# Reordering the units between the chained products of a two-layer MLP (adaLN, linear attention, Mish)

## The chip, the cores and the metric

The kernel runs on one core of a Trainium2 chip. The metric is the device time of one execution in microseconds (us), smaller being better. The engines are called PE (TensorE, matrix products), DVE (VectorE), ACT (ScalarE), POOL (GpSimd) and SP (SyncE, which only starts transfers here); each takes its instructions in the order in which the program wrote them.

## The reference

One sequence of S = 2048 rows with D = 512 columns; c is one row of 512, and silu(c) @ w_mod gives six rows of modulation (sa, ca, ga, sb, cb, gb).

```python
h = layernorm(x) * (1 + ca) + sa
x = x + ga * A(h)        # linear attention, 32 heads of 16, then wo
h = layernorm(x) * (1 + cb) + sb
x = x + gb * B(h)        # B: mish(h @ w1 + b1) @ w2, w1 512 x 1792, w2 1792 x 512
```

Everything is float32. The change touches only the second half, B, and the order of work around it.

## The kernel before, in words

**Precision.** Each float32 operand is split into a high half (fp32r) and the low rest, and a product is three matmuls: high x high, high x low, low x high (`mm3`). `split` makes the halves: ACT copies the high half (L75), and one step later DVE subtracts it from the value to give the low half (L81).

**Tiling.** The rows of x are four blocks of 512 (0 to 3). The 1792 hidden columns are 14 column tiles f of 128, taken as seven pairs g = (2g, 2g+1).

**Products of a pair.** The first layer is computed for two row blocks and the two column tiles of a pair at once, with seven products in place of eight (Strassen's scheme in Winograd's form, in the names of w1's quarters a11 .. a22, their sums s1 .. s4, the inputs' quarters b11 .. b22 and their sums t1 .. t4). One `product` (L924) is 6 matmuls of 128 x 512. Four of them accumulate one on the other in one PSUM bank `pa`, and between two of them ACT copies the bank out, so that they form a chain:

- `pair_begin`: a11 x b11 into pa (ACT copies it to u1, L940); a12 x b21 into a second bank, and DVE adds u1 to give c11 (L935).
- `pair_unit`: s1 x t1 into pc; s2 x t2 onto pa, copied to u2 (L962); s3 x t3 onto pa, copied to u3 (L967), and c22 = pc + u3; a22 x t4 onto pa, from which ACT takes mish directly (L899); s4 x b22 onto pc, and c12 = pc + u2.

A product "onto pa" can't start before ACT has copied the bank. Therefore `pair_unit` has two gaps, one ahead of s3 x t3 and one ahead of a22 x t4, in which it calls other PE work (`between[0]`, `between[1]`).

**Mish.** Of the four results of a pair, c11 and the one from pa belong to the first of the two blocks (`mish`: L899, then a split into the halves a_h and a_l), c22 and c12 to the second (`later`, `mish_b`: L922).

**Second layer.** In the first pair stage (blocks 0 and 1), `d_unit(0, f)` is the second layer of block 0 for column tile f: 12 matmuls of 128 x 512 onto four banks `oacc` (L67 to L69). `trail(f)` wraps it. The gaps of pair g hold trail(2g-1) and trail(2g), so the second of them uses the c11 of its own pair; pair 0 has an output unit of the attention, `o_unit(3, 3)`, in its first gap; trail(13) comes last. Then `second(1)` does the 14 d_units of block 1. In the last stage (blocks 2 and 3, pairs in the order 5, 6, 0, 1, 2, 3, 4) the second layer is again in seven products; `e_unit(c, n)` (12 matmuls of 256 columns) for c = 0 and 1 are the first two, and run in the gaps: e_unit(1, n-1) in the first gap of pair n, e_unit(0, n) in its second. The other products (`seventh`: m4, m6, m7, m5, m3) follow the pairs.

**The order of work.** PE's order is written out by hand. Side work is a set of generators: `spawn` adds one, and each `tick()` lets every generator do one step, in the order in which they were spawned; so the instructions of ACT, DVE, POOL and SP come between PE's at the ticks. The ones that matter here:

- `rows(g, wait)` (L588): the w1 rows of pair g. Step 1 starts two SP loads `w1p` (L593); `wait` steps later DVE makes the sums s1 to s4 (L599 to L602); then the high halves on ACT and the low halves on DVE, over three steps.
- `store_rows(g)` (L621): eight SP stores of these halves, for the last stage.
- `w2_job(f)` (L520): an SP load `w2r` (L518), after two steps DVE multiplies by gb (L526), then a split, then two or three POOL stores.
- `norm_tile(b, t)` (L764): the second layer norm of 128 rows of blocks 2 and 3. Two passes of sums on ACT (L213, L214); a step later DVE adds eps (L218) and POOL takes the power -1/2 (L192); a step later DVE makes nb (L222) and ACT applies the norm (L201); a step later POOL stores the tile.

Tiles in SBUF come from one ring of 101 slots, so a new tile also waits until the last reader of its slot is done.

**Where they are spawned before.** In the loop over the first stage's pairs: `w2_job(2g+2)` and `w2_job(2g+3)` at the head of pair g; a norm tile at the head of pairs 1 to 4 and in trails 0, 1, 3, 5, so that no pair has over two; `store_rows(g)` right after pair g, and behind it `rows(g+2, 2)`.

Of the kernel before, what the change touches and what calls it, by code (L numbers as in the profile page):

```python
# [10 lines left out]
AF = mybir.ActivationFunctionType  # L11
# [6 lines left out]
NB = S // 512  # L18
NF = F // P
# [6 lines left out]
def block_kernel(ctx: ExitStack, tc: tile.TileContext, x, wqkv, wo, w1, b1t, w2, c, wmodt, out):  # L26
# [76 lines left out]
    c0 = sb("c0")  # L103
# [408 lines left out]
    KEPT, SUMS_KEPT = 5, (3, 4)  # L512
# [75 lines left out]
    def rows(g, wait):  # L588

        r = [sb(f"w1p_{g}_{i}", F32, (P, 4, P)) for i in range(2)]  # L590
        for i in range(2):
            f = 2 * g + i
            sp.dma_start(r[i], w1[:, P * f:P * (f + 1)].rearrange("(k p) f -> p k f", p=P))  # L593
        for _ in range(wait):
            yield
        a11, a12, a21, a22 = [r[i][:, 2 * k:2 * k + 2, :] for i in range(2) for k in range(2)]
        s12, s34 = [sb(f"s{n}_{g}", F32, (P, 4, P)) for n in (12, 34)]
        s1, s2, s3, s4 = s12[:, 0:2, :], s12[:, 2:4, :], s34[:, 0:2, :], s34[:, 2:4, :]
        dve.tensor_tensor(s1, a21, a22, op=ALU.add)  # L599
        dve.tensor_tensor(s2, s1, a11, op=ALU.subtract)  # L600
        dve.tensor_tensor(s3, a11, a21, op=ALU.subtract)
        dve.tensor_tensor(s4, a12, s2, op=ALU.subtract)  # L602
        yield
        keep, todo = {}, []
        op_rows[g] = keep
        for name, v, parts in (("a1", r[0], ("a11", "a12")), ("s12", s12, ("s1", "s2")), ("s34", s34, ("s3", "s4")),
                               ("a22", a22, ("a22",))):
            half = split(f"{name}_{g}", v, keep, name)
            next(half)
            todo.append((name, half, parts))  # L610
            if len(todo) == 2:
# [113 lines left out]
    def o_unit(b, t, tag="acc"):  # L725
        p = ps(tag, f"o_{b}_{t}")
        ts = slice(P * t, P * (t + 1))
        for g in range(4):
            mm3(p, [q[:, ts] for q in qs[b, g]], ms[g], g == 0, g == 3)
        spawn(o_post(p, b, t))  # L730
# [166 lines left out]
    def mish(p, b, f):  # L897
        u = ua[f] = sb(f"u_{b}_{f}")
        act.activation(u, p, AF.Mish, bias=b1c[:, f:f + 1])  # L899
        yield from split(f"a_{b}_{f}", u, ag, (b, f))  # L900
# [23 lines left out]
    def product(g, left, right, tag="h", onto=None):  # L924

        p = onto if onto is not None else ps(tag, f"p_{left}_{g}")
        for c in range(2):
            a, b = [h[:, c, :] for h in op_a[g, left]], op_b[right, c]
            for i, (st, mv) in enumerate(((a[0], b[0]), (a[0], b[1]), (a[1], b[0]))):
                pe.matmul(p, st, mv, start=onto is None and c == 0 and i == 0, stop=c == 1 and i == 2,  # L930
                          skip_group_check=onto is not None)
        return p
# [4 lines left out]
    def pair_begin(c0, g, tags):  # L937

        u1, pa = sb(f"u1_{g}"), product(g, "a11", "b11", tags[0])
        act.activation(u1, pa, AF.Copy)  # L940
        c11 = sb(f"c11_{g}")
        add(c11, product(g, "a12", "b21", tags[1]), u1)
        return pa, c11

    def later(p, f, wait=0):
        for _ in range(wait):
            yield
        mish_b(p, f)
        yield

    def pair_unit(c0, g, between, begun=None, tags=("tp", "h", "h")):


        f = 2 * g
        u2, u3, c12, c22 = [sb(f"{n}_{g}") for n in ("u2", "u3", "c12", "c22")]
        if begun is None:
            begun = pair_begin(c0, g, tags)
            tick()
        pa, c11 = begun
        pc = product(g, "s1", "t1", tags[2])  # L960
        product(g, "s2", "t2", onto=pa)
        act.activation(u2, pa, AF.Copy)  # L962
        spawn(mish(c11, c0, f))
        tick()
        between[0]()
        product(g, "s3", "t3", onto=pa)
        act.activation(u3, pa, AF.Copy)  # L967
        add(c22, pc, u3)
        spawn(later(c22, f + 1))
        between[1]()  # L970
        m = mish(product(g, "a22", "t4", onto=pa), c0, f + 1)
        next(m)
        spawn(m)
        product(g, "s4", "b22", onto=pc)
        add(c12, pc, u2)
        spawn(later(c12, f, 1))
        tick()

    def prep_a(b, f):
        yield from split(f"a_{b}_{f}", ub.pop(f), ag, (b, f))  # L980
# [11 lines left out]
    def ahead(b, u):  # L992

        if 0 <= u - NF + 4 < NF and last_first[u - NF + 4] < 2 * KEPT:
            w2_again(last_first[u - NF + 4])
        if 0 <= u - NF + 3 < NF:
            spawn(prep_a(b, last_first[u - NF + 3]))
# [17 lines left out]
            load_wb(6)  # L1015


    def tags_of(n):
        return "tp" if n % 2 else "h", "h", "h"

    begun = {g: pair_begin(0, g, ("tp" if g else "h", "acc")) for g in range(2)}
    tick()
    o_unit(NB - 1, 2)
    tick()
    tiles = [norm_tile(b, t) for b in (2, 3) for t in range(4)]

    def trail(f):
        def unit():
            if tiles and (f == 0 or f % 2):
                spawn(tiles.pop(0))  # L1030
            d_unit(0, f, f)
            ahead(1, f)
            tick()
        return unit

    def last_o():
        o_unit(NB - 1, 3)
        tick()

    for g in range(G):  # L1040
        for f in (2 * g + 2, 2 * g + 3) if g < G - 1 else ():
            spawn(w2_job(f))
        if g == 0:
            spawn(rows(2, 3))
        if g and tiles:
            spawn(tiles.pop(0))
        pair_unit(0, g, (trail(2 * g - 1) if g else last_o, trail(2 * g)), begun.get(g), tags_of(g))
        if g < G - 2:
            store_rows(g)
        if 0 < g < G - 2:  # L1050
            spawn(rows(g + 2, 2))
        if g == G - 1:
            for n in range(8):
                load_back("n", nd, 2 + n // 4, n % 4)
    trail(NF - 1)()
    second(1, prepare)


# [45 lines left out]
    def left_trail(g):  # L1104
        yield
        yield
        yield from left_sums(g)
# [45 lines left out]
        else:  # L1153
            pool.dma_start(v, w2t[g][:, :, SUM[name], :])  # L1154

    begun = {}

    def begin_next():
        begun[1] = pair_begin(L, pairs[1], ("tp", "acc"))

    for n, g in enumerate(pairs):
        if n < 5:
            if n:
                load_rows(n)
            if n:
                load_wb(pairs[n + 1])
        if n == 5:
            load_wb(pairs[6])
            load_r(0, 0)
        if n == 6:  # L1170
            for m in pairs[:5]:
                load_wt("m4", m)
        def first(n=n):
            if n == 0:
                begin_next()
            else:
                e_unit(1, n - 1)
            tick()

        def second_gap(n=n):  # L1180
            e_unit(0, n)
            tick()

        pair_unit(L, g, (first, second_gap), begun.pop(n, None), tags_of(n))
        if n < EARLY:
            spawn(left_trail(g))

    names = ["m4", "m6", "m7", "m5", "m3"]
    units = [(name, n) for name in names for n in range(G)]
# [5 lines left out]
    for k, (name, n) in enumerate(units[:4 * G]):  # L1195
        for _ in range(2 if k in (6, 10, 14, 18) else 1):
            if ahead_of:
                nm, m = ahead_of.pop(0)
                spawn(left_prep(nm, pairs[m]))
        for _ in range(2 if k < 3 else 1):  # L1200
            if loads:
                nm, m = loads.pop(0)
                load_wt(nm, pairs[m])
        if k in (3, 8):
            load_r(k // 8, 1)
        seventh(name, tags[name], left.pop((name, pairs[n])), wt.pop((name, pairs[n])), n, G - 1)
        if n == G - 1:
            spawn(finish(name))
        tick()
        if k == 1:  # L1210
            e_unit(1, G - 1)
            spawn(finish("m2"))
            tick()
# [42 lines left out]
```

## Time and profile before

| | us |
|---|---|
| runs | 513.6, 514.48, 513.16 |
| median of the runs | 513.6 |
| profiled execution | 513.23 |
| its span | 511.4 |
| first pair stage, first product to first d_unit of block 1 | 203.36 to 324.85 |
| PE busy in the span | 493.9 |

The span runs from the first to the last instruction that the profiler recorded; the execution's own time is 1.8 us longer. Times inside the kernel are given in us from the span's start. A row of the waits view gives the engine, the waiting instruction's output and line, what released it, and the us in total, how often, and the longest. A row of the timeline gives start, duration, engine, line, operation, output and inputs, and in brackets the idle time before it and what ended that. A row of the windows view gives the stretch and its length, then the busy us of PE, PE's weight loads, DVE, ACT and POOL, the clock granted to PE, the share of time in which the DMA engines were busy, and GB/s. Matmuls are pipelined: one lasts 0.39 us in the timeline, but the next starts 0.23 us after it. Names in the rows are cut before the first number: a_2h stands for a high half named a..._2..., of w1's quarter of pair 2 as well as of a hidden tile 2.

### The profile page before, as it was taken

The numbers are of one execution on the slowest core, as the hardware profiler recorded it, in microseconds if no ns is written. First come the engines' busy times: TensorE is split into PE (matmuls) and PEld (weight loads), VectorE is DVE, ScalarE is ACT, GpSimd is POOL, SyncE is SP. The second block draws the span as 40 slices with busy tenths as digits, with TensorE's granted clock in tenths as the row PEclk, the third lists the DMA queues.
The fourth block names the chain that finished last, engine by engine and source line by source line (L and its number), as shares of the span: only waits on it lengthen the run. The fifth ranks groups of instructions, "written<-read, shape, count | busy, mean of one in ns | idle before, by whom it ended". The sixth has DMA issues, their size and how long they took to land.

```text
span 511.4 us, 7692 instructions
## 1 busy us (share of the span) xinstructions
PE 493.9 (97%) x2648; PEld 412.1 (81%) x2648; DVE 344.2 (67%) x666; ACT 295.0 (58%) x532; POOL 145.1 (28%) x246
## 2 busy tenths in 40 slices
PE   7999999999999999998999999999989999999997
PEld 6788888878788888786777778788778888899997
DVE  6896564878888679864476543779944655549862
ACT  6868683634455977457877554468245444467200
POOL 3573020000223133122533204124364231355200
PEclk9999999999999999999999999999999999999999
DMA  8724661562735135869999619879997463587612
GB/s 298 279 82 84 185 142 64 159 233 83 185 91 164 32 113 182 286 226 347 297 301 309 219 46 348 262 215 370 364 320 212 115 166 82 139 223 198 161 43 83
DMA packets 66765, 98.58 MB, mean 193 GB/s; under 512 B 7405, under 2 KB 31861, under 8 KB 66726
## 3 DMA queue, kind: packets, MB, share of 16 engines
q0 software_dynamic: 29360, 45.31, 32.2%
q1 hardware_dynamic: 37220, 52.51, 31.1%
q8 instruction: 21, 0.34, 0.3%
q10 hardware_dynamic: 146, 0.26, 0.1%
q14 instruction: 18, 0.15, 0.1%
HBM read 62.92 MB, written 33.03 MB: 188 GB/s over the span
## 4 chain that ended last, share of the span: by engine, by line
PE 81%; ACT 6%; DVE 4%; issue 4%; DMA 2%; POOL 1%; DVEq 0%; POOLq 0%; ACTq 0%
PE p_a L930 15%; PE p_s L930 6%; PE oacc L69 4%; PE oacc L68 4%; PE oacc L67 4%; PE m L69 4%; PE m L68 3%; PE m L67 3%; PE pq L67 3%; PE gacc L68 3%; PE gacc L69 3%; PE gacc L67 3%; PE pq L69 3%; PE pq L68 3%; PE o L67 3%
## 5 line engine op out<-in xcount | busy, mean ns | idle before, releaser
L935 DVE TENSOR_TENSOR c<-p_s,u 128x512 f32<-128x512 f32 x28 | 19.4, 691 | 51.6 <-PE p_s L930 33.7
L962 ACT ACTIVATE u<-p_a 128x512 f32<-128x512 f32 x14 | 8.4, 597 | 32.5 <-PE p_a L930 32.3
L922 ACT ACTIVATE ub<-c,b1c 128x512 f32<-128x512 f32 x28 | 20.1, 718 | 9.0 <-DVE c L935 9.0
L192 POOL TENSOR_TENSOR rs_n<-rs_n,half 128x1 f32<-128x1 f32 x16 | 10.8, 676 | 37.0 <-DVE rs_n L218 26.2
L1154 POOL DMA_DIRECT2D wt_m<-w2t x20 | 14.0, 704 | 25.4 <-PE p_a L930 17.3
L248 DVE SCALAR_TENSOR_TENSOR ku<-e_k,relu_k 128x512 f32<-128x512 f32 x16 | 11.0, 689 | 14.5 <-ACT relu_k L246 14.5
L586 POOL DMA_DIRECT2D w2b<-w2d x20 | 10.6, 534 | 29.5 <-PE oacc L69 8.3
L245 ACT ACTIVATE e_q<-pq 128x512 f32<-128x512 f32 x16 | 9.4, 590 | 16.5 <-PE pq L69 16.5
L788 ACT ACTIVATE hf_n<-tp_n,mc 128x512 f32<-128x512 f32 x16 | 11.7, 770 | 11.2 <-PE tp_n L786 11.2
L940 ACT ACTIVATE u<-p_a 128x512 f32<-128x512 f32 x14 | 8.3, 593 | 15.6 <-PE p_a L930 15.6
L245 ACT ACTIVATE e_k<-pk 128x512 f32<-128x512 f32 x16 | 9.6, 599 | 13.3 <-PE pk L69 13.2
L935 DVE TENSOR_TENSOR c<-p_a,u 128x512 f32<-128x512 f32 x14 | 9.7, 690 | 8.6 <-ACT u L940 5.8
L899 ACT ACTIVATE u<-p_a,b1c 128x512 f32<-128x512 f32 x14 | 9.6, 686 | 10.1 <-PE p_a L930 8.5
L694 POOL DMA_DIRECT2D rden_d<-rden x3 | 2.2, 718 | 43.4 <-DVE rden L692 43.4
L248 DVE SCALAR_TENSOR_TENSOR q<-e_q,relu_q 128x512 f32<-128x512 f32 x16 | 11.0, 688 | 4.7 <-ACT relu_q L246 4.5
L967 ACT ACTIVATE u<-p_a 128x512 f32<-128x512 f32 x14 | 8.3, 594 | 10.1 <-PE p_a L930 10.1
L580 POOL DMA_DIRECT2D wb<-w2d x14 | 9.9, 711 | 14.7 <-PE p_a L930 9.3
L201 ACT ACTIVATE x<-x,nb_x,rs_x 128x512 f32<-128x512 f32 x15 | 11.5, 810 | 3.8 <-DVE nb_x L196 3.3
L192 POOL TENSOR_TENSOR rs_x<-rs_x,half 128x1 f32<-128x1 f32 (+1 forms) x10 | 7.4, 746 | 21.2 <-DVE rs_x L187 20.4
L201 ACT ACTIVATE r<-r,nb_n,rs_n 128x512 f32<-128x512 f32 x8 | 6.5, 812 | 10.7 <-DVE nb_n L222 8.9
L718 DVE TENSOR_TENSOR r<-o,r 128x512 f32<-128x512 f32 x16 | 10.9, 679 | 2.6 <-PE o L69 2.3
L706 DVE SCALAR_TENSOR_TENSOR q<-q,rd 128x512 f32<-128x512 f32 x16 | 10.6, 686 | 2.6 <-DMA rd<-rden_d 2.5
(1426 smaller groups left out, 1941.4 us busy)
## 6 DMA issues: line engine op xcount, KB each, us to landing
wm<-in_wmodt_dram SPq DMA_DIRECT2D x24, 256.0 KB, 4.5
w2b<-w2d POOLq DMA_DIRECT2D x20, 256.0 KB, 6.1
wt_m<-w2t POOLq DMA_DIRECT2D x20, 256.0 KB, 4.0
r<-in_x_dram SPq DMA_DIRECT2D x16, 256.0 KB, 2.9
x<-in_x_dram SPq DMA_DIRECT2D x15, 256.0 KB, 4.7
w1p<-in_w_dram SPq DMA_DIRECT2D x14, 256.0 KB, 5.0
w2r<-in_w_dram SPq DMA_DIRECT2D x14, 256.0 KB, 5.3
wb<-w2d POOLq DMA_DIRECT2D x14, 256.0 KB, 4.5
```

Source lines behind the costliest of these rows:

```text
L67: pe.matmul(o, st[0], mv[0], start=start, stop=False)
L68: pe.matmul(o, st[0], mv[1], start=False, stop=False)
L69: pe.matmul(o, st[1], mv[0], start=False, stop=stop)
L192: pool.tensor_tensor(y, y, half[:, lo:hi], op=ALU.pow)
L201: act.activation(dst, t, AF.Identity, bias=nb[key, b][:, j:j + 1], scale=rs[key, b][:, j:j + 1])
L245: act.activation(e, p, AF.Exp)
L248: dve.scalar_tensor_tensor(dst, e, 1.0, r, op0=ALU.min, op1=ALU.add)
L788: act.activation(hf[b, j], p, AF.Identity, bias=mc[:, 12 + j:13 + j], scale=mc[:, 16 + j:17 + j])
L922: act.activation(u, p, AF.Mish, bias=b1c[:, f:f + 1])
L930: pe.matmul(p, st, mv, start=onto is None and c == 0 and i == 0, stop=c == 1 and i == 2, skip_group_check=onto is not None)
L935: dve.tensor_tensor(out, p, u, op=ALU.add)
L1154: pool.dma_start(v, w2t[g][:, :, SUM[name], :])
```

## The change

It has three parts.

**Units one pair back.** `pair_unit` is cut into `pair_early` (s1t1, s2t2), `pair_middle` (s3t3) and `pair_end` (a22t4, s4b22). In the first pair stage the gaps of pair g hold trail(2g-3) and trail(2g-2); trails 11, 12 and 13 come after pair 6. In the last stage the gaps of pair n hold e_unit(0, n-1) and e_unit(1, n-1), and the two e_units of the last pair run after the second of the `seventh` products.

**The first two pairs in turns.** In both stages the first two pairs (0 and 1, and 5 and 6) run in `two_pairs`, after the four products of their two `pair_begin`: s1t1 and s2t2 of the first, s1t1 of the second, s3t3 of the first, s2t2 of the second, a22t4 and s4b22 of the first, [e_unit(0, 0)], s3t3 of the second, [trail(0), or e_unit(1, 0)], a22t4 and s4b22 of the second. Between two products of one chain there is here a single product of the other pair, apart from the last gap. In the first stage both o_units stand ahead of this.

**Side work.** `rows(g+2, 2)` is spawned in the second gap of pair g, behind the d_unit, two steps sooner than before. `store_rows(0)` and `store_rows(1)` both follow `two_pairs`, 16 SP stores in a row. `w2_job(2g)` and `w2_job(2g+1)` are spawned at the head of pair g instead of a pair sooner, except those of pair 1, which keep their place. A norm tile is spawned at the head of each pair and in each trail until there are none left: two in `two_pairs`, three in pair 2, three in pair 3.

Every instruction of before is still there, and none is added; only their order changes.

```diff
-    def pair_unit(c0, g, between, begun=None, tags=("tp", "h", "h")):
...
+    def pair_early(c0, g, pa, c11, tag):
+
+        u2 = sb(f"u2_{g}")
+        pc = product(g, "s1", "t1", tag)
         product(g, "s2", "t2", onto=pa)
         act.activation(u2, pa, AF.Copy)
-        spawn(mish(c11, c0, f))
-        tick()
-        between[0]()
+        spawn(mish(c11, c0, 2 * g))
+        return pa, pc, u2
+
+    def pair_middle(g, pa, pc, u2):
+        u3, c22 = sb(f"u3_{g}"), sb(f"c22_{g}")
         product(g, "s3", "t3", onto=pa)
         act.activation(u3, pa, AF.Copy)
         add(c22, pc, u3)
-        spawn(later(c22, f + 1))
-        between[1]()
-        m = mish(product(g, "a22", "t4", onto=pa), c0, f + 1)
+        spawn(later(c22, 2 * g + 1))
+
+    def pair_end(c0, g, pa, pc, u2):
+        c12 = sb(f"c12_{g}")
+        m = mish(product(g, "a22", "t4", onto=pa), c0, 2 * g + 1)
         next(m)
         spawn(m)
         product(g, "s4", "b22", onto=pc)
         add(c12, pc, u2)
-        spawn(later(c12, f, 1))
-        tick()
+        spawn(later(c12, 2 * g, 1))
+        tick()
+
+    def pair_unit(c0, g, odd, between):
+        begun = pair_begin(c0, g, ("tp" if odd else "h", "h"))
+        tick()
+        state = pair_early(c0, g, *begun, "h")
+        tick()
+        between[0]()
+        pair_middle(g, *state)
+        between[1]()
+        pair_end(c0, g, *state)
+
+    def two_pairs(c0, g0, g1, begun, between):
+
+        s0 = pair_early(c0, g0, *begun[0], "h")
+        tick()
+        pc = product(g1, "s1", "t1", "h")
+        pair_middle(g0, *s0)
+        tick()
+        pa, c11 = begun[1]
+        u2 = sb(f"u2_{g1}")
+        product(g1, "s2", "t2", onto=pa)
+        act.activation(u2, pa, AF.Copy)
+        spawn(mish(c11, c0, 2 * g1))
+        tick()
+        pair_end(c0, g0, *s0)
+        between[0]()
+        pair_middle(g1, pa, pc, u2)
+        between[1]()
+        pair_end(c0, g1, pa, pc, u2)
...
+    begun = [pair_begin(0, g, ("tp" if g else "h", "acc")) for g in range(2)]
     tick()
-    o_unit(NB - 1, 2)
-    tick()
+    for t in (2, 3):
+        o_unit(NB - 1, t)
+        tick()
...
-    def trail(f):
+    def norm_next():
+        if tiles:
+            spawn(tiles.pop(0))
+
+    def trail(f, side=None):
         def unit():
-            if tiles and (f == 0 or f % 2):
-                spawn(tiles.pop(0))
+            norm_next()
             d_unit(0, f, f)
             ahead(1, f)
+            if side is not None:
+                spawn(side)
             tick()
         return unit
...
-    for g in range(G):
-        for f in (2 * g + 2, 2 * g + 3) if g < G - 1 else ():
+    for g in range(1, G):
+        for f in (2 * g, 2 * g + 1):
             spawn(w2_job(f))
-        if g == 0:
+        if g == 1:
             spawn(rows(2, 3))
-        if g and tiles:
-            spawn(tiles.pop(0))
-        pair_unit(0, g, (trail(2 * g - 1) if g else last_o, trail(2 * g)), begun.get(g), tags_of(g))
-        if g < G - 2:
+            norm_next()
+            two_pairs(0, 0, 1, begun, (tick, trail(0, rows(3, 2))))
+            store_rows(0)
+        else:
+            norm_next()
+            pair_unit(0, g, g % 2, (trail(2 * g - 3), trail(2 * g - 2, rows(g + 2, 2) if g + 2 < G else None)))
+        if g < KEPT:
             store_rows(g)
-        if 0 < g < G - 2:
-            spawn(rows(g + 2, 2))
...
-    trail(NF - 1)()
+    for f in (NF - 3, NF - 2, NF - 1):
+        trail(f)()
     second(1, prepare)
...
-        pair_unit(L, g, (first, second_gap), begun.pop(n, None), tags_of(n))
-        if n < EARLY:
-            spawn(left_trail(g))
+        if n == 0:
+            begun = [pair_begin(L, pairs[i], ("tp" if i else "h", "acc")) for i in range(2)]
+            tick()
+        elif n == 1:
+            two_pairs(L, pairs[0], g, begun, (gap(0, 0), gap(1, 0)))
+            for i in range(2):
+                spawn(left_trail(pairs[i]))
+        else:
+            pair_unit(L, g, n % 2, (gap(0, n - 1), gap(1, n - 1)))
+            if n < EARLY:
+                spawn(left_trail(g))
...
         if k == 1:
+            e_unit(0, G - 1)
             e_unit(1, G - 1)
             spawn(finish("m2"))
             tick()
```

More of the change, by code (lines that the diff above doesn't have):

```diff
@@ L949, in later @@
         yield
-    def pair_unit(c0, g, between, begun=None, tags=("tp", "h", "h")):
[L954 to L957, printed above, removed]
-            tick()
-        pa, c11 = begun
-        pc = product(g, "s1", "t1", tags[2])
+    def pair_early(c0, g, pa, c11, tag):
+        u2 = sb(f"u2_{g}")
+        pc = product(g, "s1", "t1", tag)
         product(g, "s2", "t2", onto=pa)
         act.activation(u2, pa, AF.Copy)
-        spawn(mish(c11, c0, f))
-        tick()
-        between[0]()
+        spawn(mish(c11, c0, 2 * g))
+        return pa, pc, u2
+    def pair_middle(g, pa, pc, u2):
+        u3, c22 = sb(f"u3_{g}"), sb(f"c22_{g}")
         product(g, "s3", "t3", onto=pa)
@@ L1015, in prepare @@
             load_wb(6)
-    def tags_of(n):
-        return "tp" if n % 2 else "h", "h", "h"
-    begun = {g: pair_begin(0, g, ("tp" if g else "h", "acc")) for g in range(2)}
+    begun = [pair_begin(0, g, ("tp" if g else "h", "acc")) for g in range(2)]
     tick()
-    o_unit(NB - 1, 2)
-    tick()
+    for t in (2, 3):
+        o_unit(NB - 1, t)
+        tick()
     tiles = [norm_tile(b, t) for b in (2, 3) for t in range(4)]
-    def trail(f):
+    def norm_next():
+        if tiles:
+            spawn(tiles.pop(0))
+    def trail(f, side=None):
         def unit():
-            if tiles and (f == 0 or f % 2):
-                spawn(tiles.pop(0))
+            norm_next()
             d_unit(0, f, f)
             ahead(1, f)
+            if side is not None:
+                spawn(side)
             tick()
         return unit
-    def last_o():
-        o_unit(NB - 1, 3)
-        tick()
-    for g in range(G):
-        for f in (2 * g + 2, 2 * g + 3) if g < G - 1 else ():
+    for g in range(1, G):
+        for f in (2 * g, 2 * g + 1):
             spawn(w2_job(f))
-        if g == 0:
+        if g == 1:
             spawn(rows(2, 3))
-        if g and tiles:
-            spawn(tiles.pop(0))
-        pair_unit(0, g, (trail(2 * g - 1) if g else last_o, trail(2 * g)), begun.get(g), tags_of(g))
-        if g < G - 2:
+            norm_next()
[5 more added lines that the diff above has]
+        if g < KEPT:
             store_rows(g)
-        if 0 < g < G - 2:
-            spawn(rows(g + 2, 2))
         if g == G - 1:
@@ L1154, in load_wt @@
             pool.dma_start(v, w2t[g][:, :, SUM[name], :])
-    begun = {}
-    def begin_next():
-        begun[1] = pair_begin(L, pairs[1], ("tp", "acc"))
     for n, g in enumerate(pairs):
@@ L1172, in block_kernel, with gap, unit @@
                 load_wt("m4", m)
[L1173 to L1177, printed above, removed]
-            tick()
-        def second_gap(n=n):
-            e_unit(0, n)
-            tick()
-        pair_unit(L, g, (first, second_gap), begun.pop(n, None), tags_of(n))
-        if n < EARLY:
-            spawn(left_trail(g))
+        def gap(c, m):
+            def unit():
+                if m >= 0:
+                    e_unit(c, m)
+                tick()
+            return unit
+        if n == 0:
+            begun = [pair_begin(L, pairs[i], ("tp" if i else "h", "acc")) for i in range(2)]
+            tick()
+        elif n == 1:
[6 more added lines that the diff above has]
+                spawn(left_trail(g))
     names = ["m4", "m6", "m7", "m5", "m3"]
```

## The prediction

> **What bounds the kernel now.** I read the busy shares first, then the chain that ended last, then TensorE's (PE's) waits, and last the timelines around those waits.
>
> ```profile
> PE 493.9 (97%) x2648; PEld 412.1 (81%) x2648; DVE 344.2 (67%) x666; ACT 295.0 (58%) x532; POOL 145.1 (28%) x246
> PE 81%; ACT 6%; DVE 4%; issue 4%; DMA 2%; POOL 1%; DVEq 0%; POOLq 0%; ACTq 0%
> ```
>
> PE is busy for 97% of the span and carries 81% of the chain, so the end moves only by what PE waits. The change moves instructions and neither adds nor removes one; its worth is waits that go less waits that come. PE's waits in the stage where the pairs of blocks 0 and 1 run (200 to 330 us; of four equal rows for a_3l to a_6l the first and the last stand here):
>
> ```profile
> PE oacc L67 <- ACT a_2h L75: 1.7, 1, 1.7
> PE oacc L69 <- DVE a_13l L81: 1.2, 1, 1.2
> PE p_a L930 <- DVE a_3l L81: 0.9, 1, 0.9
> ...
> PE p_a L930 <- DVE a_6l L81: 0.9, 1, 0.9
> PE p_s L930 <- DVE t_1l L81: 0.8, 1, 0.8
> PE p_a L930 <- ACT u L940: 0.5, 1, 0.5
> ```
>
> These nine waits sum to 7.8 us. They understate the loss, as the timeline shows. First come the bounds of the stage and of one d_unit, then a matmul before a wait and two behind it:
>
> ```profile
> 203.36 0.39 PE L930 MATMUL p_a<-b_0h,a_0h 128*128 128x512 f32 x1
> ...
> 219.45 0.39 PE L67 MATMUL oacc<-w_0h,a_0h 128*128 128x512 f32 x1
> ...
> 222.17 0.39 PE L930 MATMUL p_a<-t_0h,a_0h 128*128 128x512 f32 x1
> ...
> 285.17 0.39 PE L930 MATMUL p_a<-t_0h,a_4h 128*128 128x512 f32 x1
> ...
> 301.37 0.39 PE L930 MATMUL p_a<-t_0h,a_5h 128*128 128x512 f32 x1
> ...
> 324.85 0.39 PE L67 MATMUL oacc<-w_10h,a_10h 128*128 128x512 f32 x1
> ```
>
> ```profile
> 243.25 0.39 PE L930 MATMUL p_s<-t_1h,s_2l 128*128 128x512 f32 x1
> 244.18 0.50 PE L930 MATMUL p_a<-t_0h,s_2h 128*128 128x512 f32 x1 [0.55 <-ACT u L940]
> 244.52 0.39 PE L930 MATMUL p_a<-t_0l,s_2h 128*128 128x512 f32 x1
> ```
>
> The d_unit from 219.45 to 222.17 is 12 matmuls in 2.72 us, 0.227 each, so a product of 6 takes 1.36. The stage, 203.36 to 324.85, lasts 121.49 us and holds 49 products, 14 d_units and 2 o_units of 12: 49 x 1.36 + 16 x 2.72 = 110.2. So 11.3 us are lost, 3.5 more than the waits view lists. The second fence shows why: starts of 243.25, 244.18 and 244.52 stand 0.93 and 0.34 apart in place of 0.227 and 0.227, a loss of 0.82 for a listed 0.5; I count 0.3 to each wait beside its listed time. Between the same point of pairs 4 and 5 (285.17 and 301.37) lie 16.20 us where 7 products and 2 d_units are 14.96. That 1.24 is the price of one wait for the next pair's w1 rows, and it comes four times.
>
> In the last stage three waits concern the change. Two of the units of 12 matmuls with 256 columns start and end here, and the waits view has the second and the third:
>
> ```profile
> 376.44 0.28 PE L67 MATMUL m<-wb,a_10h 128*128 128x256 f32 x1
> 376.56 0.28 PE L68 MATMUL m<-wb,a_10h 128*128 128x256 f32 x1
> 378.60 0.39 PE L69 MATMUL m<-wb,a_10l 128*128 128x256 f32 x1 [1.76 <-DVE a_10l L81]
> ...
> 379.89 0.40 PE L930 MATMUL p_a<-t_0h,a_5h 128*128 128x512 f32 x1
> ...
> 466.57 0.28 PE L67 MATMUL m<-wt_m,l_m_5h 128*128 128x256 f32 x1
> ...
> 468.97 0.28 PE L67 MATMUL m<-wt_m,l_m_6h 128*128 128x256 f32 x1
> ```
>
> ```profile
> PE m L69 <- DVE l_m_5l L81: 0.7, 1, 0.7
> PE m L69 <- DVE a_12l L81: 0.2, 1, 0.2
> ```
>
> Undisturbed starts stand 0.12 apart (376.44 to 376.56), so twelve take 1.43; the two took 3.45 and 2.40, so 2.0 and 1.0 are lost. The third, for a_12l, is 0.2 listed and 0.3 of restart: 0.5.
>
> **The change part by part.** (1) *Units one pair back.* d_unit(0,2) waited for a_2h, made in the same pair; now trail(2) runs a pair (14.96 us of PE) later, and the 1.7 is gone. a_13l is needed by the last trail; trails 11 and 12 (5.44 us) now stand ahead of it, against 1.2. The second layer's inputs are kept one pair longer, which costs slots of the ring and no instruction. (2) *o_units first.* t_1l is needed by pair 0's s1t1. Both o_units now stand ahead of that product, 2.72 more than before against 0.8: gone. (3) *rows two steps sooner.* Each rows(g+2) is two SP loads, four DVE adds, four ACT copies and four DVE subtractions. Two steps are at least a d_unit, 2.72 us of PE, against 0.9 listed and 1.24 paid: gone four times. The loads pass ahead of store_rows on SP, which only helps them. If the cover fails, each costs 1.24 again. (4) *Last stage.* Before the first e_unit stood 7 products from 366.92 (376.44 less 9.52); now 11 do, so it comes at 381.9. a_10l came at 378.6; its subtraction now stands behind the add of c22 on DVE, which waits for s3t3 of that pair (ends 377.8) and ACT's copy, and my estimate for it from such rows is 381.3. The cover is thin; if it is gone, up to 0.5 comes back, well under the 2.5 saved. For l_m_5l DVE works through a queue that begins with the last pair's c12, and PE now has one e_unit more (1.43) in front: 1.0 falls to 0; I take 0.9.
>
> So far: 11.3 + 2.5 + 0.9 = 14.7 us go.
>
> (5) *What comes: the ACT queue inside two_pairs.* From 203.36, four begin products and two o_units end at 214.24, and the turns put s3t3 of pair 1 at 223.76 to 225.12, a d_unit to 227.84, and then a22t4 of pair 1 onto the bank that ACT must first have copied to u3. ACT runs in order. A stretch of it before gives the distances from start to start:
>
> ```profile
> 239.24 0.82 ACT L201 ACTIVATE r<-r,nb_n,rs_n 128x512 f32<-128x512 f32 x1 [2.97 <-DVE nb_n L222]
> 239.96 0.71 ACT L922 ACTIVATE ub<-c,b1c 128x512 f32<-128x512 f32 x1
> 240.57 0.67 ACT L899 ACTIVATE u<-p_a,b1c 128x512 f32<-128x512 f32 x1
> 241.27 0.63 ACT L75 ACTIVATE a_3h<-u 128x512 fp32r<-128x512 f32 x1
> 241.81 0.62 ACT L75 ACTIVATE w_4h<-w2r 128x512 fp32r<-128x512 f32 x1
> 242.33 0.62 ACT L75 ACTIVATE w_5h<-w2r 128x512 fp32r<-128x512 f32 x1
> ...
> 243.56 0.57 ACT L940 ACTIVATE u<-p_a 128x512 f32<-128x512 f32 x1
> ```
>
> The first row is the trap: the norm apply (L201) held ACT for 2.97 us until DVE had its nb. In the changed program these stand ahead of u3 of pair 1: an apply (0.72), mish and its high half for c11 (0.61 + 0.54) and for a22t4 of pair 0 (0.70 + 0.54), two w2 halves and two row halves (4 x 0.52), one mish (0.61): 5.8 us. The apply's sums end near 219.4 by the same distances; its eps waits on DVE behind c22 of pair 0 (s3t3 ends at 219.7, copy 0.6, add 0.7: 221.0), and POOL's power and DVE's nb come a step later, by my estimate at 223.7; 223.7 + 5.8 + 0.6 for the copy is 230.1. a22t4 was due at 227.84: 2.3 us, with the restart about 2.5. The bounds are 0 (nb ready three us sooner) and 4 (the 2.97 of the row, once more). I take 2.5.
>
> (6) *Norm tiles.* Two a pair become three in pairs 2 and 3. A tile is three ACT passes:
>
> ```profile
> L214 ACT ACTIVATE scrap_n<-r,sums_n 128x512 f32<-128x512 f32 x8 | 5.8, 725 | 0.3
> L213 ACT ACTIVATE scrap_n<-r 128x512 f32<-128x512 f32 x8 | 4.9, 618 | 0.0
> ```
>
> In the changed order an apply, L213 and L214 stand right ahead of u3 in both pairs, 2.1 us of ACT work that starts when the apply's nb is there. Between s3t3 and a22t4 lies one d_unit, 2.72; with the copy (0.6) ACT has nothing to spare. By the same walk I get 1.2 us in pair 2 and 1.5 in pair 3, bounds 0 and 4 each as above.
>
> (7) *SP's queue.* Both pairs' row stores, 16 in a row, now stand ahead of the loads of w2r_4 and 5. Of one set of eight the first, the slowest and the last, and the loads' median landing:
>
> ```profile
> 218.24 0.42 SPq L625 DMA_DIRECT2D rd_a<-a_1h  x1
> ...
> 220.58 1.16 SPq L625 DMA_DIRECT2D rd_s<-s_1h  x1
> ...
> 223.68 0.63 SPq L625 DMA_DIRECT2D rd_a<-a_1l  x1
> ```
>
> ```profile
> w2r<-in_w_dram SPq DMA_DIRECT2D x8, 256.0 KB, 5.9
> ```
>
> Eight take 6.1 us, sixteen 12.1; from about 225 the loads are issued at 237 and land near 243. DVE's multiplication by gb waits for them, and behind it in DVE's order stand the nb of the pair-2 tile and c22 of pair 2. That is already in the 1.2 of (6); every us beyond is one us more.
>
> With 0.13 of restart for each of three waits, 2.5 + 1.2 + 1.5 + 0.4 = 5.6 us come. From pair 4 on there are no norm tiles, and I find no new wait. **Sum:** 513.23 (span 511.4 and 1.8 around it) - 14.7 + 5.6 = 504.1; the median of the runs, 513.6, lies 0.4 above the profiled run, so **504.5 us**.
>
> Two windows of the stage, PE clock, DMA share and GB/s last:
>
> ```profile
> 236.00:252.00 16.00, 15.46 (x67) 12.21 (x66) 9.86 (x22) 11.16 (x23) 6.51 (x11) 1.00 0.98 334
> 252.00:268.50 16.50, 15.57 (x68) 12.53 (x68) 10.09 (x22) 13.64 (x28) 5.60 (x10) 1.00 0.91 305
> ```
>
> The granted clock stays 1.00 through waits of up to 1.8 us. The Trainium skill, "TensorE: Matmul & The Clock Gate", Part 1, says that PE idle for a window of about 3.4 us drops to half clock until it has been busy for another. No wait here is long enough to test it, and the waits that I forecast aren't either, so the sum is 504.5 with or without it; where a wait reaches 4 us, an estimate by that page adds 3.4 / 2 = 1.7 us for each.
>
> **The rivals.** *The new waits stay small:* if nb is early enough, ACT takes back 2 us or less, and the time is 501. For it: idle ACT time before; against it: the 2.97 row. *ACT becomes the bound in pairs 2 and 3:* ACT was busy 11.2 of 16.0 and 13.6 of 16.5 us there with two tiles a pair; a third tile (0.62 + 0.72 + 0.81 = 2.15) makes 13.3 to 15.8 of a pair that is to last 14.96 to 16.2. Then the waits of (5) to (7) go to their upper ends, 4 each, 12 in place of 5.2: 511, and halfway there 508. *It doesn't do what it says:* the rows still come late, because their ACT halves queue behind the norm passes: 4 x 1.24 back, 509.5. *Slower:* SP's order. The DMA share is already 0.91 to 0.98; if each of sixteen stores takes what the slowest of the eight did (1.16 us), w2r_4 is issued at 243.6 and lands at 249.5, and DVE holds pair 2 for 6.5 us more: 511. It decides against the change once w2r_4 lands later than 252 to 253 (the gain of 9.1 us used up past 243), with a landing of 9 us or more in place of 5.9; the rows and w2 of the next pair, behind it on SP, then repeat part of it, and 516 is my price.
>
> **How the numbers follow.** My forecast, 502.5 to 507: 0.53. Small waits, 499 to 502.5: 0.17. ACT bound, 507 to 512: 0.16. Rows still late, about 509.5: 0.04. Slower by SP, above 515: 0.06; the rest, 0.04, lies between 512 and 515. The range 500.5 to 510 leaves out some 0.06 below and 0.14 above. About 0.3% (1.5 us) is what a measurement of this kernel can tell from no change: faster by more 0.90, within it 0.04, slower by more 0.06.
>
> **What would show it.** In the profile after: no PE wait on a_2h, a_13l, t_1l nor on the a1 rows' lows (1), (2), (3); none on a_10l (4); new PE waits at a22t4 (p_a) on ACT's u of L965 in pairs 1, 2 and 3, with ACT's L201 waiting for nb just before (5), (6); DVE waiting for w2r_4's load near 243 (7); the stage about 115.8 us long. I am wrong if the new waits stand elsewhere, on DVE or a DMA above all, or if they go on past pair 3.

## The result, and the profile after

The changed kernel takes 505.34 us (four runs, 505.31 to 507.02), the kernel before 514.04 in the same comparison (four runs, 513.16 to 514.49): a ratio of 0.984, with a 95% interval of 0.982 to 0.987. The profiled execution took 505.36 us with a span of 503.6, which is 7.8 under the span before. The forecast was 504.5 in a range of 500.5 to 510.

From the page of the changed kernel, busy time by engine and the chain that ended last:

```profile
PE 492.7 (98%) x2648; PEld 414.0 (82%) x2648; DVE 343.8 (68%) x666; ACT 294.4 (58%) x532; POOL 144.8 (29%) x246
PE 87%; ACT 6%; DVE 2%; issue 2%; DMA 1%; SPq 0%; DVEq 0%; ACTq 0%
```

The same work, and PE's share of the chain has grown from 81% to 87%. The waits view of PE, from 200 us to the end, had eleven rows for the parts in question and now has one; behind it, in PE's timeline, the two ends of the first pair stage:

```profile
PE p_a L930 <- ACT u L965: 4.2, 3, 2.1
```

```profile
203.48 0.39 PE L930 MATMUL p_a<-b_0h,a_0h 128*128 128x512 f32 x1
...
320.47 0.39 PE L67 MATMUL oacc<-w_10h,a_10h 128*128 128x512 f32 x1
```

All the waits that were to go are gone: a_2h, a_13l, t_1l, the four on the rows, u in pair 2, and a_10l, a_12l and l_m_5l in the last stage. Three came, all at a22 x t4 on ACT's u3 (L965). The stage went from 121.49 to 116.99 us (forecast 115.8), with 110.2 of work as before; so it still loses 6.8. The first of the three waits, in pair 1 (timeline of PE):

```profile
227.87 0.39 PE L69 MATMUL oacc<-w_0h,a_0l 128*128 128x512 f32 x1
230.36 0.50 PE L930 MATMUL p_a<-t_0h,a_1h 128*128 128x512 f32 x1 [2.10 <-ACT u L965]
230.70 0.40 PE L930 MATMUL p_a<-t_0l,a_1h 128*128 128x512 f32 x1
...
232.03 0.63 PE L930 MATMUL p_a<-t_1h,a_1l 128*128 128x512 f32 x1
232.46 0.63 PE L930 MATMUL p_s<-b_2h,s_1h 128*128 128x512 f32 x1
...
234.59 0.39 PE L930 MATMUL p_s<-b_3h,s_1l 128*128 128x512 f32 x1
```

Something follows it that was not forecast. From 231.2 on the matmuls start 0.43 apart in place of 0.227 (232.03 to 232.46), for over 3 us. The windows view says why; the number behind the busy times is the clock granted to PE:

```profile
225.00:230.00 5.00, 3.26 (x15) 2.37 (x13) 3.84 (x8) 4.94 (x10) 2.28 (x5) 1.00 1.06 388
230.00:231.60 1.60, 1.24 (x4) 1.00 (x5) 1.26 (x3) 1.60 (x4) 1.43 (x3) 0.86 1.15 355
231.60:234.80 3.20, 3.20 (x9) 2.49 (x8) 0.63 (x2) 2.82 (x7) 0.00 (x0) 0.54 1.12 363
234.80:240.00 5.20, 5.20 (x24) 4.28 (x23) 4.42 (x11) 1.98 (x4) 1.20 (x2) 1.00 1.03 371
```

PE ran at half clock for about 3.4 us, from 0.7 us after the wait. The product with the wait's end took 2.10 and the next one 2.36 us. With a restart alone (one start after the wait at 0.34 in place of 0.227) they take 1.49 and 1.36, so this stretch at half clock, a dip from here on, cost 1.6. All four runs of the changed kernel have a mean granted clock of 0.993 to 0.997, so none is free of a dip.

### The profile page after: what moved, and what is told of

The parts are those of the page before. It is cut to its first block, busy times and chain, and to the rows that moved or that the text cites. A ratio compares the mean times of both kernels' runs of the same rounds, so it can differ in the third digit from the quotient of the medians.

```text
span 503.6 us, 7666 instructions
## 1 busy us (share of the span) xinstructions
PE 492.7 (98%) x2648; PEld 414.0 (82%) x2648; DVE 343.8 (68%) x666; ACT 294.4 (58%) x532; POOL 144.8 (29%) x246
## 4 chain that ended last, share of the span: by engine, by line
PE 87%; ACT 6%; DVE 2%; issue 2%; DMA 1%; SPq 0%; DVEq 0%; ACTq 0%
PE p_a L930 16%; PE p_s L930 6%; PE m L69 5%; PE m L68 5%; PE m L67 5%; PE oacc L69 4%; PE oacc L68 4%; PE oacc L67 4%; PE o L67 3%; PE pq L67 3%; PE gacc L68 3%; PE gacc L69 3%; PE o L69 3%; PE gacc L67 3%; PE pq L69 3%; PE pq L68 3%
## 5 line engine op out<-in xcount | busy, mean ns | idle before, releaser
L958 ACT ACTIVATE u<-p_a 128x512 f32<-128x512 f32 x12 | 7.1, 593 | 29.4 <-PE p_a L930 29.4
L940 ACT ACTIVATE u<-p_a 128x512 f32<-128x512 f32 x14 | 8.3, 596 | 17.8 <-PE p_a L930 17.8
L257 POOL DMA_DIRECT2D ku<-ku x8 | 7.2, 895 | 17.6 <-DVE ku L248 16.9
L965 ACT ACTIVATE u<-p_a 128x512 f32<-128x512 f32 x14 | 8.3, 591 | 6.2 <-PE p_a L930 6.2
```

## The experiments

All times are medians beside the kernel before on the same chip, unless a single run is named with its granted clock (the mean over a whole run). Runs of one kernel differ by up to about 1 us at the same clock (the kernel before by 2.5: 513.77 and 516.24 us at 0.996), and a dip adds to that; therefore kernels are also compared at the same clock.

**1. The rows alone**, in the kernel before:

```diff
-        pair_unit(0, g, (trail(2 * g - 1) if g else last_o, trail(2 * g)), ...
+        side = rows(g + 2, 2) if 0 < g < G - 2 else None
+        pair_unit(0, g, (trail(2 * g - 1) if g else last_o, trail(2 * g, side)), ...
...
-        if 0 < g < G - 2:
-            spawn(rows(g + 2, 2))
```

> The kernel before with one edit: rows(g+2, 2) is spawned behind the d_unit in the second gap of pair g instead of after the pair. Theory (each wait for a pair's w1 rows costs 1.24 us and comes four times): the four waits on a_3l to a_6l go and the time is 4.5 to 5.0 us below before, 509.0 to 509.5. Rival (the rows' ACT halves now stand ahead of the mish of c11 that the same pair's d_unit needs, as the units are still of the same pair): two to four new waits of about 0.5 to 1 us for a d_unit on ACT, and the gain is 3 us or less, 511 or more.

Measured: 510.14 (509.15 to 510.86), ratio 0.993 (0.991 to 0.995). At a clock of 1.00 one run took 509.15, and before 513.07 at 0.999: 3.9 less. From PE's waits in the first stage, the first and the last row:

```profile
PE oacc L67 <- ACT a_2h L75: 1.7, 1, 1.7
...
PE oacc L69 <- DVE a_4l L81: 0.3, 1, 0.3
```

The four waits are gone, but a piece comes back: d_units 4, 6, 8 and 10 take 3.39, 2.90, 2.89 and 2.83 us, where before the first took 2.99 and the others 2.72; 0.9 us in all. The one of these waits that the view lists is for the low half of the pair's own tile (a_4l, subtracted on DVE at 249.99 us), which now stands behind the rows' subtractions (247.51 and 248.11). The stage is 4.1 us shorter than before (117.39 us), which is 4 x 1.24 less the 0.9. This lies between the two theories and nearer the first. Three of the four runs were slowed by a dip; in the profiled one it follows the wait for a_10l, which is 1.76 us long in the timeline:

```profile
374.80:378.20 3.40, 3.40 (x15) 2.95 (x15) 0.26 (x1) 0.72 (x1) 3.26 (x6) 0.59 1.07 312
```

**2. The last stage alone:** the first stage as before, the last one as changed (the old `pair_unit` kept beside the new functions).

> The kernel before in the first pair stage, the changed one in the last stage (two pairs in turns, e_units one pair back). Theory (2.0 for a_10l, 0.5 for a_12l and 1.0 for l_m_5l go and nothing comes): 3.5 us below before, 510.5. Rival (the cover for a_10l is thin and l_m_5l is set by DVE's queue and not by PE's place): 1.5 to 2 us below, 512.

Measured: 509.76 (509.73 to 510.17), ratio 0.992 (0.991 to 0.994); spans 508.0 and 511.4. The 3.4 us of the forecast, and no wait of PE from 360 us to the end of the last stage. The cover that I had called thin held: a_10l's subtraction ends at 381.34 us and its first use starts at 382.20.

**3. No norm tile at the head of the turns:**

```diff
         if g == 1:
             spawn(rows(2, 3))
-            norm_next()
             two_pairs(0, 0, 1, begun, (tick, trail(0, rows(3, 2))))
```

> The changed kernel without the norm tile at the head of two_pairs (the other tiles move up, so that pair 4 gets one). Theory: the apply of that tile, which waits for nb until 223.8 us, holds ACT's queue in front of u3 of pair 1; without it u3 comes 1.4 us sooner, PE's wait there falls from 2.1 listed to about 0.7, and the half clock that follows it (granted 0.54 for 3.2 us) goes too, as the wait is now shorter than those of before that left the clock at 1.00: 1.5 + 1.6 = 3.1 us below the changed kernel, 502.2. Rival (the clock's dip belongs to the place or the load and not to the length of the wait): the dip of 1.6 us stays, 503.8. Second rival (a third cause holds u3 of pair 1, such as a DMA): no gain.

Measured: 505.47 (503.75 to 506.35), no gain over the changed kernel. (The one run near full clock, 503.75 at 0.999, stands beside 503.7 for the changed kernel without its dip of 1.6.) Yet pair 1 did what the first theory says: its gap fell from 2.49 to 0.57 us between starts, with no dip. The time was given back in pair 2. Its PE waits, then a row of DVE and one of ACT:

```profile
PE p_a L930 <- ACT u L965: 3.9, 3, 2.9
```

```profile
242.31 1.32 DVE L526 TENSOR_TENSOR w2r<-w2r,gb_bc 128x512 f32<-128x512 f32 x2 [2.09 <-DMA w2r<-in_w_dram]
243.54 0.15 DVE L222 TENSOR_TENSOR nb_n<-sums_n,rs_n 128x1 f32<-128x1 f32 x1
```

```profile
243.73 0.81 ACT L201 ACTIVATE r<-r,nb_n,rs_n 128x512 f32<-128x512 f32 x1 [2.21 <-DVE nb_n L222]
```

This is the chain of step (7): SP issues w2r_4 only behind sixteen stores, DVE waits for it with the multiplication, nb stands behind that, the apply waits for nb, and u3 stands behind the apply. PE, coming sooner, waited 2.9 us and fell to half clock for 6.7 us, from 2.3 us into the wait on. None of the three expectations had this; the place of the loss had moved.

**4. Two tiles a pair:** no norm tile at the head of pairs 2 and on (the line `norm_next()` ahead of `pair_unit` taken out), so that no apply stands right ahead of u3 there.

> The changed kernel with two norm tiles a pair in pairs 2, 3 and 4 (none at the head of the pair) in place of three in pairs 2 and 3. Theory: the apply right ahead of u3 (0.72 us, and its wait for nb) goes in pairs 2 and 3, whose waits of 1.1 and 1.6 us fall to 0.4 or less each, with at most 0.4 new in pair 4; pair 1 with its wait and its half clock stays: 1.5 to 2.2 us below the changed kernel, 503.2 to 503.8. Rival (SP's late load of w2r_4, and DVE behind it, sets pair 2): pair 2 keeps its 1.2 and only 1.2 us are won, 504.1.

Measured: 501.31 (500.94 to 502.66), ratio 0.976 (0.974 to 0.978): pairs 2 to 4 wait for nothing, and only pair 1's 2.1 us is left. Of the 4.0 us under the changed kernel 2.6 is this; the one run with a dip took 502.66. The rest is that the same wait in pair 1 brought no dip in the other three runs, which is chance. SP's queue is as it was: DVE waits 2.1 us for w2r_4 (243.32 in its timeline) and PE does not, so the late load reaches PE only through the apply. The rival falls.

**5. Both: one tile in each of trails 0 to 7, none anywhere else** (the two edits of 3 and 4).

> The changed kernel with both edits: no norm tile at the head of two_pairs and none at the head of a pair, so one tile in each of trails 0 to 7. Theory (PE's waits in pairs 1 to 3 came from the applies ahead of u3, and pair 2's only reached PE through the apply that waits for nb): pair 1 waits 0.6 or less, no other wait, 1.9 us below the two-a-pair version's undisturbed 500.94, 499.0; and with no wait over 1 us in the stage the clock stays at 0.999 or 1.00 in every run, which agree within 0.4 us. Rival (as in the version without the tile in turns, the time won in pair 1 is given back where PE meets SP's late w2r load): 500.9 or more.

Measured: 499.20 (499.06 to 499.81), ratio 0.972 (0.970 to 0.973), clock 1.0 in all four runs. From its page, and PE's waits from 195 to 505 us:

```profile
PE 490.0 (99%) x2648; PEld 412.5 (83%) x2648; DVE 343.1 (69%) x666; ACT 294.4 (59%) x532; POOL 144.6 (29%) x246
PE 94%; ACT 3%; DVE 1%; DMA 1%; issue 0%; ACTq 0%
```

```profile
PE p_a L930 <- ACT u L965: 0.2, 1, 0.2
```

It beats both kernels, and it is the base of the experiments 7 to 11.

**6. The loads of w2r_4 and 5 ahead of the sixteen stores**, in the version of 3:

```diff
             two_pairs(0, 0, 1, begun, (tick, trail(0, rows(3, 2))))
+            load_w2(4)
+            load_w2(5)
             store_rows(0)
```

> The version without the norm tile at the head of two_pairs (503.75 undisturbed) with one more edit: the loads of w2r_4 and 5 are issued ahead of the 16 row stores. Theory (sixteen stores on SP, then the load, then DVE's multiplication, nb, the apply and u3 make pair 2's 2.9 us): DVE's 2.1 us wait for the load goes, PE's wait in pair 2 falls to about 1.0, and with it the half clock: 501.9 and a granted clock of 0.998 or more. Rival (the DMA engines are full there, and the load lands no sooner or the stores pay for it later): 503.5 or more.

Measured: 505.27 (504.63 to 505.82), 504.89 in the one run at clock 1.0, which is 1.1 over the version of 3 at 0.999. In pair 2 DVE no longer waits for the load and PE's gap falls from 3.29 to 2.02 us between starts (the two w2 copies on ACT, now sooner, stand ahead of u3). But the stores are still to be issued, and the next load comes later for it: w2r_6 at 254.8 instead of 248.4. The wait moved on by a pair (PE's waits, and DVE):

```profile
PE p_a L930 <- ACT u L965: 4.9, 3, 3.1
```

```profile
259.12 1.39 DVE L526 TENSOR_TENSOR w2r<-w2r,gb_bc 128x512 f32<-128x512 f32 x2 [1.87 <-DMA w2r<-in_w_dram]
```

The rival is right: moving one transfer ahead made another one late. What helped was to cut the path by which the load reaches PE (experiments 4 and 5).

**7. No turns:** in 5's version, pairs 0 and 1 one after the other.

```diff
+            pair_unit(0, 0, 0, (last_o, trail(0)), begun[0])
...
+            pair_unit(0, 1, 1, (trail(1, rows(3, 2)), tick), begun[1])
...
-            pair_unit(0, g, g % 2, (trail(2 * g - 3), trail(2 * g - 2, ...
+            pair_unit(0, g, g % 2, (trail(2 * g - 2), trail(2 * g - 1, ...
```

> The version with tiles in trails only, but in the first stage pairs 0 and 1 run one after the other as before: one o_unit ahead, the other and trail(0) in pair 0's gaps, trail(1) in pair 1's first gap and nothing in its second; trail(2g-2) and trail(2g-1) from pair 2 on. Theory (the turns are what covers t_1l and the chains of the two pairs that have no unit of a pair back): 1.1 us for t_1l and 1.0 to 1.5 for the empty gap, 2 to 2.6 us above the version with turns, about 501.3. Rival (moving the units back and the rows sooner is the whole worth): within 0.5 us of the version with turns.

Measured: 506.31 (504.17 to 507.91), ratio 0.985 (0.981 to 0.989). At clock 1.0 one run took 504.17, 5.0 over the version with turns. PE's waits:

```profile
PE p_a L930 <- ACT u L965: 3.0, 1, 3.0
PE oacc L68 <- DVE w_12l L81: 1.2, 1, 1.2
PE p_s L930 <- DVE t_1l L81: 0.8, 1, 0.8
```

The turns are worth more than I had put: a gap with nothing in it costs not the copy alone but all that stands ahead of it on ACT, 3.0 us, and then a dip in three of four runs. The 1.2 for w_12l (1.4 with its restart) is not theirs, by my reading: the units stand one earlier here, and w2_job makes their weights no sooner. That leaves about 3.6 of the 5.0 for the turns.

**8. A long wait:** in 5's version, u3 of pair 5 copied 14 times.

```diff
-        act.activation(u3, pa, AF.Copy)
+        for _ in range(14 if g == 5 and tiles == [] and not long else 1):
+            act.activation(u3, pa, AF.Copy)
...
```

> The version with tiles in trails only, with u3 of pair 5 in the first stage copied 14 times in a row instead of once (the same copy again, so that the results are as before and PE alone is held). Theory (a PE wait of more than about 2 us brings the clock to half for some 3.4 us, in every run once the wait is over 3.4): a wait of 4.0 to 4.5 us, then matmul starts 0.43 apart for 3.4 us or more, 5.8 to 7.5 us above the version with tiles in trails only, and a granted clock of 0.997 or less in all four runs. Rival (the dip has nothing to do with the length of a wait): the wait's own 4.0 to 4.5 us and a clock of 0.999 in some of the runs.

Measured: 509.54 (508.95 to 509.88). The wait was 7.1 us, not 4.0 to 4.5: I had reckoned with idle ACT time that isn't there. 7.1 over 499.2 would be 506.3. In the profiled run (509.28) the restart and the half clock add 2.1, and some 0.6 lies ahead of the wait. The clock is at 0.993 or 0.989 in all four runs. In the windows it falls while PE waits, and stays down after:

```profile
292.00:296.00 4.00, 0.00 (x0) 0.00 (x0) 0.00 (x0) 3.79 (x7) 0.00 (x0) 0.66 0.00 0
296.00:300.00 4.00, 3.56 (x8) 2.81 (x9) 1.69 (x4) 2.63 (x5) 1.10 (x2) 0.50 0.04 11
```

**9. The rows late again**, in 5's version: `rows(g + 2, 2)` spawned after the pair.

> The version with tiles in trails only (499.2), with rows(g+2, 2) spawned after the pair again, as before. Theory (the rows' low halves are late by the same two steps wherever the units stand): four waits of 0.9 listed and 1.2 to 1.3 paid for a_3l to a_6l come back, 5.0 us, 504.2. Rival (with the units one pair back there is a d_unit more between the steps and the rows, so that their place no longer matters): 499.2 to 500.

Measured: 503.94 (503.67 to 504.06), clock 1.0 in all runs: 4.7 over 499.2. The four waits are back (first and last):

```profile
PE p_a L930 <- DVE a_3l L81: 0.9, 1, 0.9
...
PE p_a L930 <- DVE a_6l L81: 0.9, 1, 0.9
```

So the rows' two steps are the largest single part, and waits of 0.9 us left the clock alone.

**10 and 11. Waits of two and of one us:** as in 8, with 6 copies in pair 5 and 7 in pair 6, and with 4 and 6.

> The version with tiles in trails only, with u3 copied 6 times in pair 5 and 7 times in pair 6 of the first stage, so that PE waits about 2.2 and 1.9 us (0.62 us a copy, less the slack that the trace of the version with 14 copies shows), 4.5 us with the restarts: 503.7 where the clock stays. Theory (a PE wait of about 2 us halves the clock for 3.4 us in some runs, by where it falls in a window of the clock's own): some of the runs at 503.7 with a granted clock of 0.999 to 1.0, the others 1.5 to 1.8 us above for each dip, with a clock of 0.997 or 0.993. Rival (only waits over 3.4 us do that): all runs within 0.5 us of 503.7 and a clock of 0.999 or more.

> As the version with copies for two waits of about 2 us, but 4 copies in pair 5 and 6 in pair 6: waits of about 1.0 and 1.3 us, 2.6 us with the restarts, 501.8. Theory: a wait of one us leaves the clock alone, so all runs agree within 0.7 us at a granted clock of 0.999 to 1.0. Rival (any wait at PE can bring the dip): some runs 1.5 us or more above the others at 0.997.

Measured: 504.22 for the first (clock 1.0: 503.70, 503.82, 504.22; clock 0.997 and 0.996: 505.31 and 505.84), 502.03 for the second (501.59 to 502.62, clock 0.998 to 1.0). In the second the runs spread by 1.0 us, more than the 0.7 expected, but not by the clock: the slowest has 1.0. In the profiled run of the first, the wait in pair 5 (2.12 us) brought a dip, and the one in pair 6 (1.75) did not, so the rival (only waits over 3.4 us do that) falls:

```profile
291.60:295.00 3.40, 3.40 (x10) 2.63 (x9) 1.08 (x4) 2.32 (x4) 1.10 (x2) 0.51 0.20 62
...
305.00:313.00 8.00, 6.25 (x28) 4.83 (x27) 0.98 (x2) 7.16 (x12) 0.53 (x1) 1.00 0.35 119
```

## Why the prediction was right, and where it was not

**Steps (1) to (4), what goes.** Right in place and nearly in size. The rows were put at 4 x 1.24 = 5.0; experiment 9 gives 4.7. The last stage was put at 3.4; experiment 2 gives 3.4. Two things were looser than they read. The waits view lists eight waits in the stage, not nine, and about 0.9 of the 11.3 us stands in pauses too short for it, in d_units 2, 4 and 13. And the parts that the prediction names come to 9.6 with their restarts; it took the rest as gone too, without a reason for u1 in pair 2. It did go: ACT now sits idle for 1.9 us ahead of that copy (236.40 in its timeline) and makes it at once. Moving the first stage's units one pair back was not run alone; that this is what removed a_2h and a_13l rests on the two waits lists. For the o_units, experiment 7 shows it: with one of them behind s1t1 again, the wait for t_1l is back.

**Step (5), the ACT queue in pair 1.** Right to a few tenths. Three rows of ACT after:

```profile
223.80 0.82 ACT L201 ACTIVATE r<-r,nb_n,rs_n 128x512 f32<-128x512 f32 x1 [0.72 <-DVE nb_n L222]
...
229.12 0.70 ACT L922 ACTIVATE ub<-c,b1c 128x512 f32<-128x512 f32 x1
229.73 0.57 ACT L965 ACTIVATE u<-p_a 128x512 f32<-128x512 f32 x1
```

The apply waited for nb to 223.80 (forecast 223.7), the ten instructions took 5.9 us (5.8), and u3 was copied at 230.3 (230.1). A d_unit begun at 225.38 ends its 2.72 at 228.10, so PE lost 2.26 and 0.13 of restart: 2.4 for a forecast 2.5 (which holds a restart already; the sum adds it a second time). Experiment 3 shows the cause by taking the tile away.

**Step (6), three tiles a pair.** The waits of pairs 2 and 3 in PE's timeline:

```profile
248.05 0.50 PE L930 MATMUL p_a<-t_0h,a_2h 128*128 128x512 f32 x1 [0.80 <-ACT u L965]
...
264.57 0.50 PE L930 MATMUL p_a<-t_0h,a_3h 128*128 128x512 f32 x1 [1.27 <-ACT u L965]
```

By starts they cost 0.95 and 1.43 before their restarts, forecast 1.2 and 1.5. With all restarts the new waits sum to 5.2, forecast 5.6. Experiment 4 shows that the tiles at the head of the pairs make them: with two tiles a pair, the apply right ahead of u3 is gone and PE waits for nothing. The applies themselves waited for nothing there (the rows at 245.24 and 261.76 us of ACT show no idle time), so it was ACT's work in order, as the step says, and not nb.

**Step (7), SP's queue.** The order is as forecast, the size was not. The first and the last of the sixteen stores, the load behind them, and the multiplication on DVE:

```profile
223.53 0.49 SPq L625 DMA_DIRECT2D rd_a<-a_0h  x1
...
238.37 0.96 SPq L625 DMA_DIRECT2D rd_a<-a_1l  x1
239.44 1.76 SPq L518 DMA_DIRECT2D w2r<-in_w_dram  x2
```

```profile
243.76 1.37 DVE L526 TENSOR_TENSOR w2r<-w2r,gb_bc 128x512 f32<-128x512 f32 x2
```

They took 15.8 us and not 12.1, 0.99 each in place of 0.76. The DMA share is 1.02 from 223.0 to 239.4 us, and was 0.96 over the eight of before (218.0 to 224.5); whether that is the reason was not tested. By the step's own rule, that every us beyond is one us more, the load's issue at 239.4 instead of 237 should have cost PE about 2.4 us. It cost nothing: DVE did not idle for it. That is luck: DVE's other work came later as well, by my reading because of PE's lost time in pair 1 and because of ACT, whose a_3h DVE awaits to 242.55 us. In experiment 3, without the loss in pair 1, DVE waited 2.1 us for the same load and the step did decide.

**The clock.** Here the prediction failed. It said that the waits forecast are not long enough to matter and that the sum stays 504.5; behind a wait of 2.1 us came a dip that cost 1.6 more. Its ground, that the clock stays at 1.00 through waits of up to 1.8 us, holds for the one profiled run of the kernel before; 17 of its 23 runs beside the experiments have a mean clock of 0.997 or less. The sum with the measured terms closes: 14.7 go and 5.2 + 1.6 come, 7.9, against 7.8 between the spans and 7.9 between the profiled executions. By the Trainium skill, "TensorE: Matmul & The Clock Gate", Part 1, PE must be idle for a window of about 3.4 us before its clock is halved. The runs agree with the length of the dip (3.4 us in pair 1 after the change, and in experiments 1 and 10) but not with the condition: 1.76 and 2.1 us of idle were enough.

**The rivals.** The slower one (SP's order) did not decide. ACT was as busy as the second rival feared (13.1 of 16.5 us from 234.82, 14.4 of 16.1 from 251.30), but the waits stayed at 0.95 and 1.43 and did not go to 4 each. The small waits came with experiment 5 and not with the change. "It doesn't do what it says" is excluded by the waits list.

## What to carry to other kernels

When a chained accumulation waits for a copy on an in-order engine, price not the copy but all that the program has put ahead of it there, above all an instruction that itself waits for a third engine; side work is better placed behind the copy that PE needs than ahead of it. A wait that goes may only make way for the next queue, so try the relief of two places together before judging either: compared without dips, the edits of experiments 3 and 4 gave nothing and about 2.6 us alone, and 4.5 together (499.2 beside 503.7). And count a PE wait of about two us as more than two: in some runs here the clock was at half behind it.

## What the runs showed of the hardware

For waits of about two us a dip came in some runs of a kernel and not in others. The longest PE waits from 195 us on (as the waits view lists them) and the runs whose mean granted clock was under 0.998:

| kernel | longest waits, us | runs with a dip |
|---|---|---|
| experiment 5 | 0.2 | 0 of 4 |
| experiment 9 | 0.9 (four) | 0 of 4 |
| experiment 11 | 1.1 | 0 of 5 |
| experiment 2 | 1.7 | 1 of 4 |
| before, beside the experiments | 1.8, 1.7 | 17 of 23 |
| experiment 1 | 1.8, 1.7 | 3 of 4 |
| experiment 4 | 2.1 | 1 of 4 |
| experiment 10 | 2.1, 1.8 | 2 of 5 |
| the changed kernel | 2.1, 1.3 | 4 of 4 |
| experiments 3, 6 and 7 | 2.9 to 3.1 | 9 of 12 |
| experiment 8 | 7.1 | 4 of 4, at 0.993 or less |

No kernel whose waits were 1.1 us or less had a dip, and none whose longest was 1.7 or more was free of them. A dip lasted 3.4 us, or about twice that in experiments 3 and 8, and cost 0.6 us (before, medians of 513.3 without and 513.9 with) to 1.7 (the changed kernel, 505.3 and 507.0, where the clock of one run, 0.993, fits a second one). A guess that would fit: a fixed window of 3.4 us decides, and PE must be idle for about half of it (the shortest wait with a dip behind it in a trace is 1.76 us). In the traces the dips begin within the waits of 2.9, 3.0 and 7.1 us (experiments 3, 7 and 8), and 0.6 to 1.1 us behind the waits of 1.76, 2.1 and 3.1 (experiment 1, the changed kernel, experiments 10 and 6). No run was made to show it, and most rows above have few runs.
